# Weight pairs of the experts: seven block products in a row, then the pair's second product

## The chip, the cores and the metric

The kernel runs on 1 core of one Trainium2 chip. The metric is device microseconds (us) of that core for one execution; lower is better. TensorE (PE) multiplies, VectorE (DVE), ScalarE (ACT) and GpSimd (POOL) do the rest, SyncE (SP) issues DMAs. [...]

## The reference

Three stages, all in fp32: attention in which a query sees only keys of its own hash bucket (2 x 8 heads, 768 tokens, head size 64); a feed-forward layer `h = x @ w_in`, `g = h * tanh(softplus(h))`, `g @ w_out` (1536 tokens, 512 to 2048 to 512); and a mixture of 8 experts:

```python
for e in range(E):                       # E = 8
    h = np.maximum(x @ w1[e], 0.0)       # 1536 x 512 @ 512 x 1024
    ye = h @ w2[e]                       # 1536 x 1024 @ 1024 x 512
    out += P[:, e:e + 1] * ye            # P: gate probabilities, normalized 8 times
```

The change is in the last stage alone, in experts 1 to 7.

## The kernel before, in words

Every fp32 operand is split in two parts of type fp32r, hi and lo, and a product is three matmuls: hi with hi, hi with lo, lo with hi. Expert 0 runs with the feed-forward layer in an older scheme (lines 787 to 823: `up`, `down`). Experts 1 to 7 run in "units". A unit `u` is one half of the tokens (768, `g`), one expert `e`, and one of its four pairs `k` of 128-wide chunks of the hidden size; there are 2 x 7 x 4 = 56 units. Units 4n to 4n+3 are one expert on one half of the tokens.

The first product of a unit is a 2 x 2 block product (two chunks of the hidden size by two groups of 384 tokens) made by seven block products instead of eight (`PRODUCTS`, steps s = 0 to 6). Each is six matmuls of 128 x 128 by 128 x 384 (line 1122). They go to two PSUM banks, `bank[0]` and `bank[1]`, in turn: steps 0, 2, 4, 6 write the first, steps 1, 3, 5 the second, and only steps 0, 1 and 4 start a new sum. So what a step leaves in its bank must have been read before the step after next adds to the same bank. These reads are in `post(u, s)`: ACT copies step 0's result to `p1` (line 1152); DVE adds `p1` to the bank after steps 1 and 3 (`u`, `v`) and makes three of the four blocks of the hidden layer after steps 4, 5, 6 (`c22`, `c21`, `c12`, `total`, line 1142); block 11 is what step 2 leaves in the first bank, as it stands. For each block, ACT makes `hi = relu(c)` (`rounded`, line 1130) and DVE makes `lo = max(c, 0) - hi` (`rest`, line 1135). For block 11 both read the bank itself.

The second product of a unit takes the four hi/lo blocks as stationary operands and the unit's second weights (`w` or `ww`) as moving ones: 36 matmuls of 128 x 128 by 128 x 512 (`second_mm`, line 1185) into six PSUM banks `y`, one for each 128 tokens. A bank collects the four units of an expert; then `gather` (line 1195, DVE) adds it, times the gate probability, to `acc`. The last expert's results go out by DMA.

The order of the work is written out by hand at the end of the function. Before the change, the seven products of unit `u` alternate with the second product of unit `u - 1`: one block product, five or six matmuls of the second product, the next block product, and so on. Around each step stand `post`, the gathers that are due, and `jobs`: the conversions of the next weights (`unit_a`, `unit_s`, `unit_w`: hi on ACT, lo on POOL, and the sums of blocks on POOL), the scaling of `acc` by the first expert's probability in units 0 to 3 (`scale_first`), and the token-side factors for the second half of the tokens (`raw_next`, `parts_next`, units 18 to 28). An engine executes its instructions in the order in which they are issued here; PSUM tiles and SBUF tiles carry the waits between engines. In unit 0 there is no earlier unit, so its seven products stand in a row.

Of the kernel before, what the change touches and what calls it, by code (L numbers as in the profile page):

```python
# [24 lines left out]
NF = FE // P  # L25
# [27 lines left out]
def f32(t):  # L53
    return t[:].bitcast(F32)
# [3 lines left out]
def lsh_attention_moe_kernel(  # L58
# [13 lines left out]
    nc = tc.nc  # L72
# [24 lines left out]
    NU = 2 * (E - 1) * NF // 2  # L97

    def unit(u):
        g, x = divmod(u, NU // 2)  # L100
        return g, 1 + x // (NF // 2), x % (NF // 2)
# [667 lines left out]
    hps, hid, yps = {}, {}, {}  # L769
# [6 lines left out]
    def step(n):  # L776
        g, tb, i = steps[n]
        return g, tb, i, i == GROUPS[g][0], i == GROUPS[g][-1]
# [236 lines left out]
    t0 = start_e + 12  # L1015
# [31 lines left out]
    for i in range(RING_A + NX + 1, NW):  # L1047
        need = free[i - RING] + 1 if i >= RING else 0
        if NATT <= i < N64:
            nd = max(nd, free_dec.get(i - NDEC, 0))  # L1050
            for j in range(2):
                d = int(nd)
# [5 lines left out]
        t = nxt  # L1058
# [5 lines left out]
    for n in range(NST + LAG):  # L1064
# [6 lines left out]
        first = n >= LAG and step(n - LAG)[0] < NG and step(n - LAG)[4]  # L1071
# [16 lines left out]


    pool = lambda name, **kw: ctx.enter_context(tc.tile_pool(name=name, reuse_waits="tile", **kw))  # L1090
    wb_p, c_p, h_p = pool("wb", bufs=1), pool("c", bufs=1), pool("hid", bufs=2)
    ps_u = pool("ps_u", bufs=1, space=bass.MemoryType.PSUM)
    ps_z = pool("ps_z", bufs=1, space=bass.MemoryType.PSUM)
    wbuf.append(dict(
        s=wb_p.tile([P, 2, 1024], F32R, name="ws"), a=wb_p.tile([P, 2, 768], F32R, name="wa"),
# [3 lines left out]
    def weight(u, name, m, kc):  # L1099
        x, b = ("s", int(name[1]) - 1) if name[0] == "S" else ("a", ("A11", "A12", "A22").index(name))  # L1100
        return wbuf[u % 2][x][:, m, b * 256 + kc * P:b * 256 + (kc + 1) * P]

    def moving(u, name, m, kc):
        g = unit(u)[0]
        if name[0] == "T":
            return factor_t(g, int(name[1]), m, kc)
        return (xh, xl)[m][:, (int(name[1]) - 1) * (KC // 2) + kc, tokens(g, int(name[2]) - 1)]

    PRODUCTS = (
        ("A11", "B11", 0, True), ("S2", "T2", 1, True), ("A12", "B21", 0, False), ("S3", "T3", 1, False),  # L1110
        ("S1", "T1", 0, True), ("A22", "T4", 1, False), ("S4", "B22", 0, False),
    )
    bank, val, hid_u, y_t = {}, {}, {}, {}

    def product(u, s):
        a, b, x, first = PRODUCTS[s]
        if first:
            bank[x] = ps_u.tile([P, 512], F32, tag=f"u{(u + x) % 2}", name="u")[:, :HALF]
        n = 0
        for kc in range(KC // 2):  # L1120
            for m, mm in ((0, 0), (0, 1), (1, 0)):
                nc.tensor.matmul(bank[x], weight(u, a, m, kc), moving(u, b, mm, kc), start=(first and n == 0), stop=(n == 5), skip_group_check=not first)  # L1122
                n += 1

    def temp(tag, bufs=1):
        return c_p.tile([P, HALF], F32, tag=tag, name=tag, bufs=bufs)

    def rounded(u, c, src):
        hi = h_p.tile([P, HALF], F32R, tag=f"h{c}", name="gh")
        nc.scalar.activation(hi, src, AF.Relu)  # L1130
        hid_u[u, c] = [hi]

    def rest(u, c, src):
        lo = h_p.tile([P, HALF], F32R, tag=f"l{c}", name="gl")
        nc.vector.scalar_tensor_tensor(  # L1135
            out=lo, in0=src, scalar=0.0, in1=f32(hid_u[u, c][0]), op0=ALU.max, op1=ALU.subtract
        )
        hid_u[u, c].append(lo)

    def total(tag, x, y, bufs=1):  # L1140
        t = val[tag] = temp(tag if bufs == 1 else "c", bufs)
        nc.vector.tensor_add(t, x, y)  # L1142
        return t


    def post(u, s):
        a, b = bank[0], bank.get(1)
        if s == 0:
            if u:
                rest(u - 1, "12", val["c12"])  # L1150
            val["p1"] = temp("p1")
            nc.scalar.copy(val["p1"], a)
        elif s == 1:
            total("u", b, val["p1"])
        elif s == 2:
            rounded(u, "11", a)
            rest(u, "11", a)
        elif s == 3:
            total("v", b, val["p1"])
        elif s == 4:  # L1160
            rounded(u, "22", total("c22", a, val["v"], 2))
        elif s == 5:
            rounded(u, "21", total("c21", b, val["p1"], 2))
            rest(u, "22", val["c22"])
        else:
            rounded(u, "12", total("c12", a, val["u"], 2))
            rest(u, "21", val["c21"])

    def second(u):
        r = []  # L1170
        if u == NU - 1:
            order = [(c, t) for t in range(6) for c in (("11", "21") if t < 3 else ("22", "12"))]
        else:
            order = [(c, t) for c, t0 in (("11", 0), ("22", 3), ("21", 0), ("12", 3)) for t in range(t0, t0 + 3)]
        for n, (c, t) in enumerate(order):
            r += [(c, t, m, all(x[1] != t for x in order[:n]), all(x[1] != t for x in order[n + 1:])) for m in range(3)]
        return r

    def second_mm(u, c, t, m, first, last):
        g, e, k = unit(u)  # L1180
        if first and m == 0 and k == 0:
            y_t[t] = ps_z.tile([P, 512], F32, tag=f"z{t}", name="y")
        hi, lo = hid_u[u, c]
        y = wbuf[u % 2]["w"][:, int(m == 1), (int(c[0]) - 1) * 512:int(c[0]) * 512]
        nc.tensor.matmul(  # L1185
            y_t[t], (hi, hi, lo)[m][:, t % 3 * P:(t % 3 + 1) * P], y,
            start=(k == 0 and first and m == 0), stop=(k == NF // 2 - 1 and last and m == 2),
        )
        if last and m == 2 and k == NF // 2 - 1:
            done.append((g, e, t))  # L1190

    def gather(g, e, t):
        i = g * 6 + t
        dst = acc[:, i // KC, i % KC, :]
        nc.vector.scalar_tensor_tensor(
            out=dst, in0=y_t[t], scalar=prob[:, i, e:e + 1], in1=dst, op0=ALU.mult, op1=ALU.add
        )
        if e == E - 1:
            nc.sync.dma_start(out=out[i * P:(i + 1) * P, :], in_=dst)

    jobs = {}

    def job(u, s, f, *args):
        jobs.setdefault((u, s), []).append(lambda: f(*args))

    for u in range(NU):
        if u:
            job(u, 0, unit_w_hi, u)
            job(u, 0, unit_w_lo, u)
        if u == 0:  # L1210
            for s, f in enumerate((unit_a_hi, unit_a_lo, unit_s_hi, unit_s_lo)):
                job(u, s // 2, f, u + 1)
        elif u + 1 < NU:
            job(u, 1, unit_s, u + 1)
            job(u, 2, unit_a_hi, u + 1)
            job(u, 3, unit_s_hi, u + 1)
            job(u, 3, unit_s_lo, u + 1)
            job(u, 4, unit_a_lo, u + 1)
    for i in range(NT):
        job(i // 3, 1 + 2 * (i % 3), scale_first, i)  # L1220

    half = NU // 2

# [5 lines left out]
        parts_t(1, k, kc, held.pop((k, kc)))  # L1229

    for x in range(8):
        job(half - 10 + x, 3, raw_next, (1, 2, 4, 3)[x % 4], x // 4)
        if x % 4 == 2:
            job(half - 10 + x, 5, parts_next, 2, x // 4)
    for x, (u, s) in enumerate(((-1, 4), (-1, 5), (-1, 6), (0, 0), (0, 1), (0, 2))):
        job(half + u, s, parts_next, (3, 1, 4)[x // 2], x % 2)

    done = []
    for u in range(NU + 1):
        downs = second(u - 1) if u else []  # L1240
        for s in range(7):
            if u < NU:
                product(u, s)
            elif s == 0:
                rest(u - 1, "12", val["c12"])
            for x in downs[len(downs) * s // 7:len(downs) * (s + 1) // 7]:
                second_mm(u - 1, *x)
                if u == NU:
                    for d in done:
                        gather(*d)  # L1250
                    done.clear()
            if u < NU:
                post(u, s)
            for d in done:
                gather(*d)
            done.clear()
            for f in jobs.pop((u, s), []):
                f()
    assert not jobs, jobs.keys()


# [48 lines left out]
```

## Time and profile before

| what | value |
|---|---|
| runs before | 1592.61 us median of 3 (1591.12 to 1593.59) |
| span of the profiled execution, first to last instruction | 1591.4 us |
| TensorE busy | 1556.9 us, 98% of the span |
| TensorE weight loads | 1343.6 us, 84% (overlap the matmuls) |
| DVE, ACT, POOL busy | 54%, 40%, 55% |
| units of experts 1 to 7 | 704.0 us to about 1588 us of the span |

The profile gives no other time of its execution than the span. The units take more than half of it. A row of a list of instructions gives the start in us from the span's start, the duration, the engine, the line, what it writes and reads, and how many were merged in it; an idle time and its releaser stand in brackets.

### The profile page before, as it was taken

To read this page: it belongs to the slowest core of one execution; us is meant where nothing else is said; L and a number is where in the kernel's file an instruction comes from. 1 tells how busy PE (TensorE), PEld (TensorE's weight loads), DVE (VectorE), ACT (ScalarE), POOL (GpSimd) and SP (SyncE) were. 2 spreads that over 40 slices of the span, in tenths; PEclk is the share of its full clock that TensorE was granted. 3 is DMA by queue.
4 is the path that set the end of the run, shared out by engine and by line. 5 is a ranking of instruction groups with operands and counts; after the bars stand their busy time and mean duration, and the time that the engine had idled before them with its cause. 6 is when DMAs were issued, how large, how long until landed. Compare 5 with 4: busy or idle time off the path is not lost.

```text
span 1591.4 us, 20016 instructions
## 1 busy us (share of the span) xinstructions
PE 1556.9 (98%) x7407; PEld 1343.6 (84%) x7407; DVE 862.9 (54%) x1480; ACT 641.2 (40%) x1167; POOL 873.6 (55%) x697
## 2 busy tenths in 40 slices
PE   7889999999999999999999999999999999999999
PEld 5777777888888878888998998898898899899897
DVE  7999998687884222674433334455534243334243
ACT  4767766644333322223333333333333333333331
POOL 4787877442424240126565656666666666665652
PEclk9999999999999999999999999999999999999999
DMA  6645442022222010001222222222232222222221
GB/s 145 172 112 132 115 139 73 15 80 67 67 66 67 14 54 1 14 27 67 67 67 67 66 67 67 68 66 71 75 105 62 72 67 66 67 67 67 67 67 40
DMA packets 62641, 113.44 MB, mean 71 GB/s; under 512 B 18176, under 2 KB 18920, under 8 KB 62544
## 3 DMA queue, kind: packets, MB, share of 16 engines
q1 hardware_dynamic: 62544, 112.17, 23.9%
q8 instruction: 58, 0.95, 0.3%
q14 instruction: 39, 0.32, 0.1%
HBM read 89.22 MB, written 3.15 MB: 58 GB/s over the span
## 4 chain that ended last, share of the span: by engine, by line
PE 87%; DVE 10%; issue 1%; ACT 1%; DMA 1%; SPq 0%; DVEq 0%; ACTq 0%
PE y L1185 29%; PE u L1122 26%; PE y L823 12%; PE h L787 4%; PE h L789 4%; PE h L788 4%; PE pav L487 3%; DVE mx L399 3%; PE ps L385 1%; PE pst L437 1%; PE pst L438 1%; DVE col L404 0%; DVE bit L343 0%; DVE bit L337 0%; DVE xu L516 0%
## 5 line engine op out<-in xcount | busy, mean ns | idle before, releaser
L1185 PE MATMUL y<-w,gh 128*128 128x512 f32 x672 | 218.5, 393 | 0.0
L1185 PE MATMUL y<-ww,gh 128*128 128x512 f32 x672 | 218.1, 393 | 0.0
L1130 ACT ACTIVATE gh<-c 128x384 fp32r<-128x384 f32 x168 | 88.0, 526 | 278.4 <-DVE c L1142 278.4
L449 POOL TENSOR_TENSOR plo<-p,ph 128x384 fp32r<-128x384 f32 x128 | 142.3, 1122 | 68.9 <-ACT ph L446 37.9
L1185 PEld LDWEIGHTS y<-ww,gh 128*128 128x128 f32 x672 | 124.8, 188 | 18.2
L1185 PEld LDWEIGHTS y<-w,gh 128*128 128x128 f32 x672 | 124.8, 188 | 17.8
L1011 POOL TENSOR_TENSOR w<-stage,w 128x1024 fp32r<-128x1024 f32 x28 | 67.1, 2395 | 132.5 <-ACT w L1007 132.5
L1011 POOL TENSOR_TENSOR ww<-stage,ww 128x1024 fp32r<-128x1024 f32 x28 | 67.1, 2395 | 127.2 <-ACT ww L1007 127.2
L1185 PE MATMUL y<-w,gl 128*128 128x512 f32 x336 | 132.2, 394 | 0.0
L1185 PE MATMUL y<-ww,gl 128*128 128x512 f32 x336 | 132.2, 393 | 0.0
L1004 POOL TENSOR_TENSOR w<-sraw,w 128x1024 fp32r<-128x1024 f32 x28 | 67.4, 2407 | 107.3 <-ACT w L1000 107.3
L157 POOL TENSOR_TENSOR stage<-stage,sgn 128x512 f32<-128x512 f32 x32 | 46.6, 1455 | 119.8 <-DVE sgn L155 48.3
L1142 DVE TENSOR_TENSOR u<-u,p 128x384 f32<-128x384 f32 x56 | 31.2, 557 | 146.6 <-PE u L1122 146.6
L823 PE MATMUL y<-gh,w 128*128 128x512 f32 x336 | 110.2, 389 | 0.0
L443 ACT ACTIVATE p<-pst 128x384 f32<-128x384 f32 x192 | 92.9, 488 | 35.4 <-PE pst L438 31.2
L787 PE MATMUL h<-xh,w 128*128 128x512 f32 x252 | 99.5, 395 | 0.0
L788 PE MATMUL h<-xl,w 128*128 128x512 f32 x252 | 98.2, 390 | 0.0
L789 PE MATMUL h<-xh,w 128*128 128x512 f32 x252 | 98.1, 389 | 0.0
L1135 DVE SCALAR_TENSOR_TENSOR gl<-c,gh 128x384 fp32r<-128x384 f32 x168 | 94.2, 560 | 6.1 <-ACT gh L1130 0.2
L399 DVE TENSOR_REDUCE mx<-ps 128x1 f32<-128x768 f32 x95 | 89.9, 946 | 13.5 <-PE ps L385 12.9
L1130 ACT ACTIVATE gh<-u 128x384 fp32r<-128x384 f32 x56 | 27.5, 491 | 161.6 <-PE u L1122 161.6
L1135 DVE SCALAR_TENSOR_TENSOR gl<-u,gh 128x384 fp32r<-128x384 f32 x56 | 31.2, 557 | 109.8 <-ACT gh L1130 109.7
(246 smaller groups left out, 4060.7 us busy)
## 6 DMA issues: line engine op xcount, KB each, us to landing
stage<-in_w_dram SPq DMA_DIRECT2D x152, 512.0 KB
raw<-in_qk_dram SPq DMA_DIRECT2D x13, 384.0 KB
wx<-hi SPq DMA_DIRECT2D x20, 192.0 KB
vt<-in_v_dram SPq DMA_DIRECT2D x16, 192.0 KB
out_dram<-acc SPq DMA_DIRECT2D x12, 256.0 KB
zq<-hi SPq DMA_DIRECT2D x11, 192.0 KB
ak<-hi SPq DMA_DIRECT2D x11, 192.0 KB
zq<-lo SPq DMA_DIRECT2D x11, 192.0 KB
```

Of the source, the lines that this page charges most:

```text
L399: nc.vector.tensor_reduce(out=m[:, t:t + 1], in_=s_t[t][:, :, :HALF], axis=AX.XY, op=ALU.max)
L443: nc.scalar.activation(p_t[u, c], st_t.pop((u, c))[:, :HALF], AF.Exp, scale=0.125)
L449: (nc.gpsimd if e == "P" else nc.vector).tensor_sub(out, in0, in1)
L787: nc.tensor.matmul(t, wt[:, 0, f], xh[:, kc, c], start=(kc == 0), stop=False)
L788: nc.tensor.matmul(t, wt[:, 0, f], xl[:, kc, c], start=False, stop=False)
L789: nc.tensor.matmul(t, wt[:, 1, f], xh[:, kc, c], start=False, stop=(kc == KC - 1))
L823: nc.tensor.matmul(yps[j], x, y, start=(head and m == 0), stop=(tail and m == 2))
L1011: nc.gpsimd.tensor_sub(y[:, 1, :], t, f32(y)[:, 0, :])
L1122: nc.tensor.matmul(bank[x], weight(u, a, m, kc), moving(u, b, mm, kc), start=(first and n == 0), stop=(n == 5), skip_group_check=not first)
L1130: nc.scalar.activation(hi, src, AF.Relu)
L1135: nc.vector.scalar_tensor_tensor(out=lo, in0=src, scalar=0.0, in1=f32(hid_u[u, c][0]), op0=ALU.max, op1=ALU.subtract)
L1185: nc.tensor.matmul(y_t[t], (hi, hi, lo)[m][:, t % 3 * P:(t % 3 + 1) * P], y, start=(k == 0 and first and m == 0), stop=(k == NF // 2 - 1 a ...
```

## The change

The seven products of a unit stand in a row (`for s in range(NP1)`), each followed by its `post`; then come the 36 matmuls of the same unit's second product in four runs of nine. Block 11 is no longer turned into its lo part from the bank: DVE copies the bank to `c11` in SBUF (`tensor_copy`), and all four `rest` follow step 6. The order within the second product is changed, so that matmuls with hi parts of blocks 11 and 22 come first. Conversions of weights move: `unit_w` of the next unit to the front of a unit (step -1), the others behind the products (`NP1 + 1`), and so do `scale_first` and the token-side factors. The hidden blocks and the sums have one buffer in place of two.

```diff
-    wb_p, c_p, h_p = pool("wb", bufs=1), pool("c", bufs=1), pool("hid", bufs=2)
+    wb_p, c_p, h_p = pool("wb", bufs=1), pool("c", bufs=1), pool("hid", bufs=1)
...
         if s == 0:
-            if u:
-                rest(u - 1, "12", val["c12"])
             val["p1"] = temp("p1")
             nc.scalar.copy(val["p1"], a)
         elif s == 1:
             total("u", b, val["p1"])
         elif s == 2:
             rounded(u, "11", a)
-            rest(u, "11", a)
+            val["c11"] = temp("c11")
+            nc.vector.tensor_copy(val["c11"], a)
         elif s == 3:
             total("v", b, val["p1"])
         elif s == 4:
-            rounded(u, "22", total("c22", a, val["v"], 2))
+            rounded(u, "22", total("c22", a, val["v"]))
         elif s == 5:
-            rounded(u, "21", total("c21", b, val["p1"], 2))
-            rest(u, "22", val["c22"])
+            rounded(u, "21", total("c21", b, val["p1"]))
         else:
-            rounded(u, "12", total("c12", a, val["u"], 2))
-            rest(u, "21", val["c21"])
+            rounded(u, "12", total("c12", a, val["u"]))
+            for c in ("11", "22", "21", "12"):
+                rest(u, c, val["c" + c])
...
+        order = [(c, t, m) for c in ("11", "22") for t in tiles[c] for m in (0, 1)]
         if u == NU - 1:
...
+            for c, d in (("11", "21"), ("22", "12")):
+                for t in tiles[c]:
+                    order += [(c, t, 2)] + [(d, t, m) for m in range(3)]
         else:
...
+            order += [(c, t, 2) for c in ("11", "22") for t in tiles[c]]
+            order += [(c, t, m) for c in ("21", "12") for t in tiles[c] for m in (0, 1)]
+            order += [(c, t, 2) for c in ("21", "12") for t in tiles[c]]
...
+    for f in (unit_a_hi, unit_a_lo, unit_s_hi, unit_s_lo):
+        job(0, 0, f, 1)
+    for u in range(NU - 1):
+        job(u, -1 if u else 1, unit_w_hi, u + 1)
+        job(u, -1 if u else 1, unit_w_lo, u + 1)
+        if u + 2 < NU:
+            job(u, 0 if u else 1, unit_s, u + 2)
+            job(u, NP1 + 1, unit_a_hi, u + 2)
+            job(u, NP1 + 1, unit_s_hi, u + 2)
+            job(u, NP1 + 1, unit_a_lo, u + 2)
+            job(u, NP1 + 1, unit_s_lo, u + 2)
     for i in range(NT):
-        job(i // 3, 1 + 2 * (i % 3), scale_first, i)
+        job(i // 3, NP1 + 1 + i % 3, scale_first, i)
...
+    for x in range(6):
+        job(half - 1, NP1 - 1 + x // 2, parts_next, (3, 1, 4)[x // 2], x % 2)
...
+    for u in range(NU):
+        run_jobs(u, -1)
+        for s in range(NP1):
+            product(u, s)
+            post(u, s)
+            run_jobs(u, s)
+        downs = second(u)
+        for r in range(NRUN):
+            for x in downs[len(downs) * r // NRUN:len(downs) * (r + 1) // NRUN]:
+                second_mm(u, *x)
+                if u == NU - 1:
+                    settle()
+            settle()
+            run_jobs(u, NP1 + r)
```

`settle` issues the gathers that are due, `run_jobs` the jobs of a step.

## Rows read from the trace of the kernel before

**Rows 1.** The page: busy time and share of each engine.

```profile
PE 1556.9 (98%) x7407; PEld 1343.6 (84%) x7407; DVE 862.9 (54%) x1480; ACT 641.2 (40%) x1167; POOL 873.6 (55%) x697
```

**Rows 2.** Busy time by stretch: the units with both products, with PEclk and DMA.

```profile
712.86:1580.00 867.14, 867.14 (x4295) 781.26 (x4295) 351.61 (x614) 296.14 (x501) 541.28 (x433) 1.00 0.21 67
```

**Rows 3.** The chain that ended last: start, duration, engine, line, matmuls merged.

```profile
693.29 10.88 PE y L823 x48
704.17 2.12 PE u L1122 x12
...
727.38 1.39 PE y L1185 x6
729.82 1.16 PE y L1185 x5
732.04 1.16 PE y L1185 x5
...
1562.31 1.39 PE y L1185 x6
1578.06 9.58 PE y L1185 x42
```

**Rows 4.** Timeline of unit 0's products, steps 1 to 5, and a later conversion.

```profile
705.08 1.20 PE L1122 MATMUL u<-tw,w 128*128 128x384 f32 x6
705.28 0.48 ACT L1152 COPY p<-u 128x384 f32<-128x384 f32 x1 [8.32 <-PE u L1122]
...
706.12 0.33 PE L1122 MATMUL u<-xh,wx 128*128 128x384 f32 x1
...
706.39 0.56 DVE L1142 TENSOR_TENSOR u<-u,p 128x384 f32<-128x384 f32 x1 [1.48 <-PE u L1122]
...
707.16 1.23 PE L1122 MATMUL u<-tw,w 128*128 128x384 f32 x6
707.43 0.49 ACT L1130 ACTIVATE gh<-u 128x384 fp32r<-128x384 f32 x1
...
708.02 0.56 DVE L1135 SCALAR_TENSOR_TENSOR gl<-u,gh 128x384 fp32r<-128x384 f32 x1
...
708.64 1.01 PEld L1122 LDWEIGHTS u<-tw,w 128*128 128x128 f32 x6 [0.57 <-DVE gl L1135]
...
709.81 1.20 PE L1122 MATMUL u<-tw,wx 128*128 128x384 f32 x6
...
714.54 1.05 ACT L1007 CAST ww<-stage 128x1024 fp32r<-128x1024 f32 x1
```

**Rows 5.** DVE's groups by line and shape: busy us, mean ns, idle before.

```profile
L1195 DVE SCALAR_TENSOR_TENSOR acc<-y,prob,acc 128x512 f32<-128x512 f32 x84 | 59.1, 742 | 4.1 <-PE y L1185 4.1
...
L446 DVE CAST ph<-p 128x384 fp32r<-128x384 f32 x33 | 16.3, 493 | 3.4 <-ACT p L443 2.2 <-PE pav L487 0.9
...
L975 DVE TENSOR_TENSOR tw<-t,tw 128x384 fp32r<-128x384 f32 x14 | 11.8, 845 | 8.0 <-ACT tw L974 8.0
...
L854 DVE COPY lgs<-lg 16x512 f32<-16x512 f32 x3 | 2.0, 679 | 9.0 <-PE lg L849 9.0
```

**Rows 6.** The attention's PSUM tile `pav`: one reader; who waited for this tile's instructions (us, times).

```profile
L497 ACT COPY xu<-pav x32: 459/475/482, 39.9 to 300.0; 64x384 f32<-64x384 f32 x32
...
  ACT xu L497: 23.5, 21
```

**Rows 7.** Timeline: one instance of the two reads of `pav`.

```profile
85.80 0.58 DVE L495 STREAM_TRANSPOSE rs<-pav 64x384 f32<-64x384 f32 x1
...
86.42 0.47 ACT L497 COPY xu<-pav 64x384 f32<-64x384 f32 x1 [1.02 <-DVE rs L495]
```

**Rows 8.** Timeline: two gathers in a row, and the first gather of the last unit.

```profile
1022.77 1.40 DVE L1195 SCALAR_TENSOR_TENSOR acc<-y,prob,acc 128x512 f32<-128x512 f32 x2
...
1580.44 0.39 PE L1185 MATMUL y<-ww,gl 128*128 128x512 f32 x1
...
1580.87 0.75 DVE L1195 SCALAR_TENSOR_TENSOR acc<-y,prob,acc 128x512 f32<-128x512 f32 x1 [1.06 <-PE y L1185]
```

More of the change, by code (lines that the diff above doesn't have):

```diff
@@ L1138, in rest, with total @@
         hid_u[u, c].append(lo)
-    def total(tag, x, y, bufs=1):
-        t = val[tag] = temp(tag if bufs == 1 else "c", bufs)
+    def total(tag, x, y):
+        t = val[tag] = temp(tag)
         nc.vector.tensor_add(t, x, y)
@@ L1160, in post @@
         elif s == 4:
-            rounded(u, "22", total("c22", a, val["v"], 2))
+            rounded(u, "22", total("c22", a, val["v"]))
         elif s == 5:
-            rounded(u, "21", total("c21", b, val["p1"], 2))
-            rest(u, "22", val["c22"])
-        else:
-            rounded(u, "12", total("c12", a, val["u"], 2))
-            rest(u, "21", val["c21"])
+            rounded(u, "21", total("c21", b, val["p1"]))
+        else:
+            rounded(u, "12", total("c12", a, val["u"]))
+            for c in ("11", "22", "21", "12"):
+                rest(u, c, val["c" + c])
     def second(u):
-        r = []
+        tiles = {c: range(3 * int(c[1]) - 3, 3 * int(c[1])) for c in ("11", "22", "21", "12")}
+        order = [(c, t, m) for c in ("11", "22") for t in tiles[c] for m in (0, 1)]
         if u == NU - 1:
-            order = [(c, t) for t in range(6) for c in (("11", "21") if t < 3 else ("22", "12"))]
-        else:
[L1174 to L1177, printed above, removed]
+            for c, d in (("11", "21"), ("22", "12")):
+                for t in tiles[c]:
+                    order += [(c, t, 2)] + [(d, t, m) for m in range(3)]
+        else:
+            order += [(c, t, 2) for c in ("11", "22") for t in tiles[c]]
+            order += [(c, t, m) for c in ("21", "12") for t in tiles[c] for m in (0, 1)]
+            order += [(c, t, 2) for c in ("21", "12") for t in tiles[c]]
+        return [
+            (c, t, m, all(x[1] != t for x in order[:n]), all(x[1] != t for x in order[n + 1:]))
+            for n, (c, t, m) in enumerate(order)
+        ]
     def second_mm(u, c, t, m, first, last):
         g, e, k = unit(u)
-        if first and m == 0 and k == 0:
+        if first and k == 0:
             y_t[t] = ps_z.tile([P, 512], F32, tag=f"z{t}", name="y")
@@ L1186, in second_mm @@
             y_t[t], (hi, hi, lo)[m][:, t % 3 * P:(t % 3 + 1) * P], y,
-            start=(k == 0 and first and m == 0), stop=(k == NF // 2 - 1 and last and m == 2),
+            start=(k == 0 and first), stop=(k == NF // 2 - 1 and last),
         )
-        if last and m == 2 and k == NF // 2 - 1:
+        if last and k == NF // 2 - 1:
             done.append((g, e, t))
@@ L1204, in job @@
         jobs.setdefault((u, s), []).append(lambda: f(*args))
[L1206 to L1218, printed above, removed]
+    NP1 = len(PRODUCTS)
+    NRUN = 4
+    for f in (unit_a_hi, unit_a_lo, unit_s_hi, unit_s_lo):
[9 more added lines that the diff above has]
+            job(u, NP1 + 1, unit_s_lo, u + 2)
     for i in range(NT):
-        job(i // 3, 1 + 2 * (i % 3), scale_first, i)
+        job(i // 3, NP1 + 1 + i % 3, scale_first, i)
     half = NU // 2
@@ L1231, in lsh_attention_moe_kernel, with settle, run_jobs @@
     for x in range(8):
-        job(half - 10 + x, 3, raw_next, (1, 2, 4, 3)[x % 4], x // 4)
+        job(half - 10 + x, NP1 + 1, raw_next, (1, 2, 4, 3)[x % 4], x // 4)
         if x % 4 == 2:
-            job(half - 10 + x, 5, parts_next, 2, x // 4)
-    for x, (u, s) in enumerate(((-1, 4), (-1, 5), (-1, 6), (0, 0), (0, 1), (0, 2))):
-        job(half + u, s, parts_next, (3, 1, 4)[x // 2], x % 2)
+            job(half - 10 + x, NP1 + 2, parts_next, 2, x // 4)
+    for x in range(6):
+        job(half - 1, NP1 - 1 + x // 2, parts_next, (3, 1, 4)[x // 2], x % 2)
     done = []
[L1239 to L1258, printed above, removed]
+    def settle():
+        for d in done:
+            gather(*d)
+        done.clear()
+    def run_jobs(u, s):
+        for f in jobs.pop((u, s), []):
+            f()
+    for u in range(NU):
[12 more added lines that the diff above has]
+            run_jobs(u, NP1 + r)
     assert not jobs, jobs.keys()
```

## The prediction, made before the changed kernel was run

> **What bounds the kernel now.** I read the page first: TensorE is busy 98% of the span, no other engine over 55% [rows 1]. [...] A unit begins every 15.753 us (727.38 to 1562.31 us is 53 units) [rows 3]. Inside it, five matmuls of the second product take 1.16 us (0.231 each), and the next five begin 2.22 us later, so a block product between them takes 1.06 us [rows 3]. Where 512-wide matmuls stand long in a row, 48 take 10.88 us, 0.2267 each, and of the last 42 the 36 behind the last switch take 9.58 - 6 x 0.231 = 8.19 us [rows 3]. Two block products in a row without a wait take 2.08 us, 1.04 each (705.08 to 707.16) [rows 4]; 12 right behind a switch take 2.12 [rows 3]. A switch between the two kinds thus costs some 0.04 us, and the kernel now makes fourteen per unit.
>
> Fourth, the timeline of unit 0, which has no earlier unit's second product: it is the changed order of products already, in small, and it is there that I look for gaps.
>
> **The change part by part.**
>
> *Grouping.* A unit's TensorE work becomes 7 x 1.04 + 0.04 + 8.19 = 15.51 us against 15.753: 0.243 less. Between the start of unit 1's products and the last second product there are 55 such units: -13.4 us. Bounds: nothing, if the spacing stays as it is; -17, if the switches left cost nothing (15.44 us per unit).
>
> *Cover taken from the reads of the banks.* Before, a reader of a bank had the next product and ten matmuls, some 3.4 us, until the bank was written again. Now it has one product, 1.04 us, and the weight load of the writer wants to start when the sixth matmul does, 0.87 us after the product. Unit 0 shows a read by DVE: the product ended at 706.12, the add began 0.27 later and took 0.56; a weight load behind such a DVE instruction starts 0.06 after it (708.02 + 0.56 to 708.64) [rows 4]. That is 0.89: 0.02 late. I take 0.05 per unit for the two steps of this kind (s = 3 behind `u`, s = 6 behind `c22`): +2.8 us; 0 to 0.1 per unit as bounds.
>
> *The copy of block 11.* After step 2 two engines read the first bank: ACT for hi, then DVE, now by a copy that needs nothing of ACT's result. Do they run side by side? The attention has such a pair: DVE transposes one half of `pav`, ACT copies the other half into another tile. ACT waited for DVE 21 times of 32 at this tile, 23.5 us in all [rows 6], and an instance shows it: DVE 85.80 to 86.38, ACT from 86.42 after 1.02 us idle [rows 7]. Neither reads what the other writes; what they share is the bank. So reads of a bank by two engines go one after the other, in program order, 0.04 apart, and the copy will stand behind the ReLU. [...]
>
> The chain after step 2: ReLU from +0.27 for 0.49 (707.43, product end 707.16) [rows 4], DVE from +0.80, copy 0.55, weight load of step 4 at +1.41. The copy is worked out from DVE's copy of 512 fp32 out of PSUM, 0.679 us [rows 5], by columns between 0.51 (all of it scaled) and 0.56 (like the add); the farthest rows, an SBUF source with 0.493 [rows 5], would give 0.06 less. In unit 0 the same chain, with `rest` as its third link and DVE 0.06 late, put that load at +1.48, and steps 3 and 4 took 709.81 - 707.16 = 2.65 us for 2.08 [rows 4]: 0.57 lost. At +1.41 it is 0.50. In 42 of the 55 units: +21.0 us. Bounds 0.40 to 0.57 per unit: +17 to +24.
>
> *Gathers.* An expert's six banks now all finish with the last six matmuls of a fourth unit, so its six gathers stand in a block in DVE's queue, ahead of the next unit's `u`. The first can begin 0.43 us after the start of its bank's last matmul (1580.44 to 1580.87) [rows 8], which is 6 x 0.227 = 1.36 before the end: at -0.93. Two take 1.40 [rows 8], one 0.742 [rows 5], so they follow at 0.66 and DVE is free at +3.03; `u` could have begun at 2.11 + 0.27 = 2.38. It ends at 3.59, the load of step 3 starts at 3.65 in place of 2.98, and 0.63 us is lost by the measure of unit 0. While TensorE waits there, the copy of block 11 catches up (3.95 to 4.50, load 4.56, wanted at 4.6), so 0.63 takes the place of 0.50. 13 times: +8.2 us. Bounds 0.50 (the gathers hidden behind the copy's stall) to 1.0.
>
> *Conversions and the rest.* `unit_w` of the next unit opens a unit on ACT, in front of `p1`. It may start when the second product before has read its buffer, about +0.2, and takes 1.05 [rows 4]; `p1` then runs 1.29 to 1.77, and the load of step 2 can start at 1.83, wanted at 1.94. Hidden, with 0.1 to spare; each 0.1 beyond costs 5.5 us. The four `rest` and `c12` take five times 0.56 behind the products, ready by +3.1, while the first lo part is wanted after 12 matmuls (2.7 us) and it is done at 1.4: hidden by the second product. The other conversions have 8.2 us of second product and a unit more before they are read. The single buffers are written again only after the second product that read them: nothing. `parts_next` of the change of token half puts six subtractions of 0.85 us [rows 5] (1.13 in the worst stretch) behind the rests of unit 27, ahead of its gathers, and makes `u` 1 to 2.6 us later still: +2, once. In unit 0 the `scale_first` that held up its products goes, but three conversions now stand before the ReLU on ACT: about +0.1 together.
>
> *Sum* against the span of 1591.4: -13.4 + 2.8 + 21.0 + 8.2 + 2.0 + 0.1 = +20.7, span 1612.1. The runs' median lies 1.2 above that span; with the same 1.2 the time is 1613.3, said as 1613 us.
>
> **The rivals.**
>
> *A: the copy runs beside the ReLU.* For it: neither needs the other. Against it: the 21 waits [rows 6]. The 21.0 go; 55 x (0.05 - 0.243) + 8.2 + 2.0 - 0.5 = -0.9: 1592 us, no change, between 1586 and 1597. It decides from 0.08 us per unit: a copy that makes the load later than that turns no change into slower. This is the only case not slower that I can work out.
>
> *B: the spacing does not depend on the neighbours,* so grouping gives nothing: 1613 + 13 = 1626 us. Against it: 0.231 and 0.2267 in the same profile [rows 3]. [...]
>
> *C: `p1` comes late,* since ACT's conversion starts later than +0.2. For it: only 0.1 us to spare. At 0.2 beyond that, 55 x 0.2 = 11: 1624 us.
>
> **How the numbers follow.** Forecast 0.78, A 0.12, B 0.05, C 0.05. The forecast's own range is 1602 to 1622: the copy's bounds (-4, +3), the gathers (-2, +5), the grouping's lower end (-4), the half's change. From 1600 to 1624 lie some 0.74 of the forecast's 0.78 and C's 0.05, about 0.8 in all, and A and B are left out; that is the range. What a measurement of this kernel tells from no change is about 0.2%, 3.2 us. Slower by more than that: the forecast, B, C and a little of A, 0.89. Within it 0.07, faster 0.04, both from A.
>
> **What would show it.** In the profile after: products 0 to 2 at 1.04 us each; between the first matmuls of steps 3 and 5 some 2.6 us in place of 2.08, with a wait of TensorE for the DVE copy `c11`, whose start is at the ReLU's end + 0.04; the second product at 0.227 per matmul; a unit every 16.0 us; six gathers in a block at every fourth unit and the wait there at step 3, for `u`. Wrong if the copy starts with the ReLU (A), if 512-wide matmuls still stand 0.231 apart (B), if step 2 waits for ACT (C), or if the gathers begin later than 0.9 us before the end of a second product.

## The result, and the profile after

| | median us | runs | against the kernel before, 95% interval |
|---|---|---|---|
| before | 1591.86 | 4 (1590.89 to 1593.59) | |
| after | 1606.03 | 4 (1605.9 to 1608.38) | 1.0089 [1.0076, 1.0103] |

The change costs 14.2 us, where the forecast was 20.7: slower, by the mechanism forecast, and inside the range; the forecast cost was about 1.4 times the measured one. The profiled execution after has a span of 1606.6 us against 1591.4, so the trace shows 15.2; 15.0 of it lies in the units.

The page after, busy time and share, answers to [rows 1]:

```profile
PE 1560.1 (97%) x7407; PEld 1335.7 (83%) x7407; DVE 957.3 (60%) x1536; ACT 642.4 (40%) x1167; POOL 875.9 (55%) x697
```

The same 7407 matmuls; DVE has 56 instructions more, the copies, and is busy 94 us longer. The stretch of the units, one row for [rows 2]:

```profile
712.86:1594.00 881.14, 869.13 (x4290) 771.94 (x4289) 446.89 (x668) 295.68 (x499) 541.78 (x433) 1.00 0.21 66
```

In this stretch TensorE, which had no gap before (busy 867.14 of 867.14 us, [rows 2]), now has 12 us of 881 without a matmul. The stalls worked out below are longer: a matmul's record (0.33 us) lasts past the start of the next where none waits (0.17 us, a sixth of 1.04), and so covers the first part of a gap. The granted clock is 1.00 in both stretches. The chain that ended last shows the new order and its price; it answers to [rows 3] (start, duration, engine, line, count):

```profile
1002.18 8.20 PE y L1189 x36
1010.38 3.16 PE u L1122 x18
1014.75 3.43 PE u L1122 x18
1018.76 2.97 DVE gl L1135 x4
1025.42 3.12 DVE acc L1199 x5
1029.89 4.46 PE u L1122 x24
1034.35 8.20 PE y L1189 x36
```

The second product takes 8.20 us for 36 matmuls (8.19 forecast). The first unit's chain runs 18 matmuls (steps 0 to 2) from 1010.38 to 1013.54, and goes on at 1014.75: between them step 3 (1.04 us) and a wait. In the next unit, behind an expert's last, the chain runs through four `rest` and the gathers on DVE, and the wait is one step earlier. The timeline of the first one, against [rows 4]:

```profile
1012.33 0.33 PE L1122 MATMUL u<-xh,wa 128*128 128x384 f32 x1
...
1012.59 0.56 DVE L1142 TENSOR_TENSOR u<-u,p 128x384 f32<-128x384 f32 x1 [2.57 <-PE u L1122]
...
1013.21 1.07 PEld L1122 LDWEIGHTS u<-tw,ws 128*128 128x128 f32 x6
1013.37 1.23 PE L1122 MATMUL u<-tw,ws 128*128 128x384 f32 x6
1013.62 0.49 ACT L1130 ACTIVATE gh<-u 128x384 fp32r<-128x384 f32 x1 [1.60 <-PE u L1122]
...
1014.14 0.56 DVE L1155 COPY c<-u 128x384 f32<-128x384 f32 x1 [0.99 <-ACT gh L1130]
...
1014.75 1.33 PE L1122 MATMUL u<-tw,ws 128*128 128x384 f32 x6 [0.16 <-DVE c L1155]
...
1015.93 1.20 PE L1122 MATMUL u<-tw,wa 128*128 128x384 f32 x6
```

The first three rows are the read of step 1's result: its product ends at 1012.33, the add into `u` begins 0.26 us later, and the weight load that waits for it comes 0.06 after its end, in time. Step 2's product ends where step 3 starts, at 1013.37. ACT's ReLU ends at 1014.11, DVE, idle for 0.99 us, begins its copy 0.03 later, and step 4 starts at 1014.75, 0.05 after the copy. Steps 3 and 4 take 2.56 us instead of 2.08. And the timeline behind an expert's last unit, against [rows 8]:

```profile
1025.34 4.03 DVE L1199 SCALAR_TENSOR_TENSOR acc<-y,prob,acc 128x512 f32<-128x512 f32 x6
...
1029.30 0.54 DVE L1142 TENSOR_TENSOR u<-u,p 128x384 f32<-128x384 f32 x1
...
1029.89 2.38 PE L1122 MATMUL u<-tw,w 128*128 128x384 f32 x12 [0.37 <-DVE u L1142]
1030.13 0.56 DVE L1155 COPY c<-u 128x384 f32<-128x384 f32 x1 [0.29 <-ACT gh L1130]
```

Six gathers in a block, 4.03 us; `u` begins when they are through, 3.09 us into the unit (3.03 forecast). Steps 3 and 4 then run as 12 without a gap: the copy's wait is covered. The list of who waited for whom, from 720 us on, so behind the first unit, has two rows with a weight load of TensorE (waiter, releaser, us in total, times, longest):

```profile
PEld u L1122 <- DVE c L1155: 20.4, 42, 0.5
PEld u L1122 <- DVE u L1142: 9.3, 13, 1.5
```

Before, the same list had no row of TensorE. These are the two terms of the sum: the copy in 42 units and the gathers in 13.

### The profile page after: what moved, and what is told of

Read it like the earlier page. It is cut to its first block, busy times and chain, and to the rows that moved or that the text cites. A ratio compares the mean times of both kernels' runs of the same rounds, so it can differ in the third digit from the quotient of the medians.

```text
span 1606.6 us, 20403 instructions
## 1 busy us (share of the span) xinstructions
PE 1560.1 (97%) x7407; PEld 1335.7 (83%) x7407; DVE 957.3 (60%) x1536; ACT 642.4 (40%) x1167; POOL 875.9 (55%) x697
## 4 chain that ended last, share of the span: by engine, by line
PE 80%; DVE 14%; ACT 2%; DMA 2%; issue 1%; SPq 0%; POOL 0%; ACTq 0%; DVEq 0%
PE y L1189 27%; PE u L1122 21%; PE y L823 12%; PE h L787 4%; PE h L789 4%; PE h L788 4%; DVE acc L1199 3%; PE pav L487 3%; DVE mx L399 2%; DVE c L1155 2%; ACT gh L1130 1%; PE ps L385 1%; PE pst L437 1%; PE pst L438 1%; DVE bit L343 0%
## 5 line engine op out<-in xcount | busy, mean ns | idle before, releaser
L1135 DVE SCALAR_TENSOR_TENSOR gl<-c,gh 128x384 fp32r<-128x384 f32 x224 | 168.5, 814 | 0.0
L1189 PE MATMUL y<-ww,gh 128*128 128x512 f32 x672 | 163.4, 391 | 0.0
L1189 PE MATMUL y<-w,gh 128*128 128x512 f32 x672 | 162.6, 391 | 0.0
L987 POOL TENSOR_TENSOR wa<-stage,wa 128x512 fp32r<-128x512 f32 x28 | 38.5, 1374 | 109.6 <-ACT wa L982 85.8
L1122 PE MATMUL u<-tw,w 128*128 128x384 f32 x420 | 85.8, 344 | 8.5 <-DVE u L1142 5.1
L1122 PE MATMUL u<-tw,ws 128*128 128x384 f32 x420 | 88.0, 344 | 4.6 <-DVE c L1155 4.6
L1122 PEld LDWEIGHTS u<-tw,w 128*128 128x128 f32 x420 | 72.5, 188 | 17.5 <-DVE u L1142 9.3
```

What stands on the lines that cost most here:

```text
L1135: nc.vector.scalar_tensor_tensor(out=lo, in0=src, scalar=0.0, in1=f32(hid_u[u, c][0]), op0=ALU.max, op1=ALU.subtract)
L1189: nc.tensor.matmul(y_t[t], (hi, hi, lo)[m][:, t % 3 * P:(t % 3 + 1) * P], y, start=(k == 0 and first), stop=(k == NF // 2 - 1 and last),)
```

## The experiments

The theory: two engines read a PSUM bank one after the other, by waits that come with the program's PSUM tiles, and in the tight order this puts the ReLU in front of the read that step 4 waits for. The rivals: the copy's own latency, a wait for data, or the grouping itself. Ratios are against runs of the kernel before on the same chip; "the stage" is the stretch from the first block product to the start of the last matmul, 883.2 us before and 898.2 after, which leaves out what varies ahead of the units: their first product begins between 701.8 and 704.4 us in these profiles, with the same code in front of it.

**DVE copies first, and the ReLU reads the copy.**

```diff
-            rounded(u, "11", a)
             val["c11"] = temp("c11")
             nc.vector.tensor_copy(val["c11"], a)
+            rounded(u, "11", val["c11"])
```

> The changed kernel (1606.0 us) with step 2's two reads of the first bank in the other order: DVE copies the bank to c11, and the ReLU of block 11 reads c11. Theory (reads of a bank by two engines go in series, and the ReLU in front of the copy is what makes step 4 late): the bank is free after one read, the load of step 4 at +0.87 us where it is wanted, steps 3 and 4 take 2.08 us in place of 2.54 in 42 units, so -0.46 x 42 = -19.5: 1586.5 us, below the kernel before. At the 13 units behind gathers nothing changes. Rival (the time of step 4 is the copy's own latency on DVE, whoever reads first): 1606 us, steps 3 and 4 still 2.5 us.

Measured: 1587.08 us, 0.9962 [0.995, 0.9975]; the stage is 20.3 us shorter than after the change, 1.4 of it in unit 0. Of the two waits one is left:

```profile
PEld u L1122 <- DVE u L1142: 9.3, 13, 1.5
```

One read of the bank, 0.56 us, fits into a product of 1.04 us here; two, 0.49 and 0.56 us, did not. The rival falls: DVE's copy is as long as before (0.56 us on average in the profile of both edits below, which has the same order) and no longer in the way.

**Both reads from the bank, DVE's first.** This tells whether the gain came from the order or from the number of reads.

```diff
-            rounded(u, "11", a)
             val["c11"] = temp("c11")
             nc.vector.tensor_copy(val["c11"], a)
+            rounded(u, "11", a)
```

> The changed kernel (1606.0 us) with DVE's copy of the bank first and the ReLU second, both still reading the bank, so neither has data of the other. Theory (two engines read one bank in series, in program order): the chain is as long as before, 0.25 + 0.56 + 0.04 + 0.49 + 0.06 = 1.40 us after step 2, steps 3 and 4 take 2.54 us and the time is 1606 us. Rival 1 (the reads may overlap, and the first edit's gain came from DVE starting first): 1587 us as with the ReLU reading c11. Behind gathers the copy now waits for u, and the ReLU behind it: +0.5 x 13 = up to 6 us more, 1612.

Measured: 1606.15 us, 1.0084 [1.007, 1.0098], as after the change. The timeline of one unit:

```profile
1012.20 1.23 PE L1122 MATMUL u<-tw,ws 128*128 128x384 f32 x6
1012.39 0.56 DVE L1154 COPY c<-u 128x384 f32<-128x384 f32 x1 [0.42 <-PE u L1122]
...
1013.05 0.49 ACT L1130 ACTIVATE gh<-u 128x384 fp32r<-128x384 f32 x1 [2.20 <-DVE c L1154]
...
1013.59 1.31 PE L1122 MATMUL u<-tw,ws 128*128 128x384 f32 x6 [0.17 <-ACT gh L1130]
```

ACT's input has been there since the product ended, at 1012.20, and ACT is idle; it starts at 1013.05, 0.10 after DVE's copy ends, though it reads nothing that DVE wrote. The order is turned round, and the stall has the same size. The extra loss behind gathers did not come: the units there are as long as after the change.

**Block 11's lo part from the bank, as in the kernel before.**

```diff
             rounded(u, "11", a)
-            val["c11"] = temp("c11")
-            nc.vector.tensor_copy(val["c11"], a)
+            rest(u, "11", a)
...
-            for c in ("11", "22", "21", "12"):
+            for c in ("22", "21", "12"):
```

> The changed kernel with block 11's lo part made by DVE from the bank behind the ReLU, as in the kernel before, and no copy. Theory (the copy waits for the ReLU by the bank anyhow, so that it needs nothing of its result gives nothing): 1606.0 us within 1, steps 3 and 4 still 2.54 us. Rival (the copy runs at least partly beside the ReLU and saves time against the old lo part): 0.2 us or more per unit slower, 1614 us.

Measured: 1611.62 us, 1.0117 [1.0103, 1.0131]: neither number. An ordinary unit's products take 7.79 us on average against 7.77, as the theory has it: an instruction that needs the ReLU's result starts when one that doesn't need it did (0.03 us behind the ReLU's end, 1029.93 to 1029.96 us in one unit, as the copy did after the change). The time is 5.6 us longer than after the change, but the profiled execution after was the slowest of its four, and from profile to profile the stage is 3.8 us longer; what else the time holds stays open. Of the 3.8, 3.2 lie in one place, the first unit of the second half of the tokens (11.1 us of products in place of 7.9). The timeline just before it:

```profile
1151.25 3.73 DVE L975 TENSOR_TENSOR tw<-t,tw 128x384 fp32r<-128x384 f32 x2 [1.21 <-ACT tw L974]
...
1151.85 2.72 POOL L1004 TENSOR_TENSOR ws<-sraw,ws 128x1024 fp32r<-128x1024 f32 x1
...
1154.90 4.03 DVE L1198 SCALAR_TENSOR_TENSOR acc<-y,prob,acc 128x512 f32<-128x512 f32 x6
...
1158.86 0.54 DVE L1142 TENSOR_TENSOR u<-u,p 128x384 f32<-128x384 f32 x1
...
1159.45 3.00 PE L1122 MATMUL u<-tw,w 128*128 128x384 f32 x9 [1.94 <-DVE u L1142]
```

With DVE's list 0.6 us shorter, two subtractions from SBUF fell beside a long POOL instruction and took 3.73 us, where after the change they took 1.84. The gathers began 1.4 us later than there and `u` with them, and TensorE's wait for `u` grew by 1.6 us. That is half of the 3.2. The other half is the clock: behind this wait of some 2 us, nine matmuls take 3.00 us, 0.32 from one to the next in place of 0.173, and by stretch (PEclk is the third number from the end):

```profile
1160.00:1163.00 3.00, 3.00 (x11) 3.00 (x11) 0.56 (x1) 0.00 (x0) 0.79 (x2) 0.50 0.86 247
1164.00:1167.00 3.00, 3.00 (x17) 2.70 (x16) 2.06 (x5) 1.90 (x4) 0.00 (x0) 1.00 0.00 0
```

The granted clock was 0.50 there, and 1.00 again behind it. In the profiles before and after it is 1.00 in every 15 us of the units. No run shows why it fell here.

**A second ReLU of the bank.**

```diff
             rounded(u, "11", a)
+            nc.scalar.activation(temp("dup"), a, AF.Relu)
             val["c11"] = temp("c11")
```

> The changed kernel (1606.0 us) with a second ReLU of the same bank into an unused tile between the ReLU of block 11 and DVE's copy; the output is the same. Theory (the copy waits for ACT's last read of the bank): the load of step 4 comes 0.40 us later, +0.40 x 42 = 16.8 us, and behind gathers, where the copy has some 0.1 us to spare, +0.3 x 13 = 4: 1627 us; steps 3 and 4 together 2.95 us in place of 2.54. Rival (the copy waits for something else, or only for its own data): 1606 us.

Measured: 1625.21 us, 1.0207 [1.0193, 1.0221], 19 us more than the change for 21 expected. An ordinary unit is 0.38 longer on average, one behind gathers 0.22.

**Gathers spread over the second product.**

```diff
-        if u == NU - 1:
+        if unit(u)[2] == NF // 2 - 1:
             for c, d in (("11", "21"), ("22", "12")):
```

> The changed kernel with the order of the last unit's second product used in every fourth unit, so that an expert's six banks finish 0.9 us apart from the 16th matmul on and the gathers no longer stand in a block. Theory (the gathers' stall takes the place of the copy's, and does not add to it): behind an expert the products fall from 7.92 to 7.78 us, 12 times, and from 8.82 once: -0.14 x 12 - 1.0 = -2.7: 1603.3 us. Rival (the gathers' 0.6 us adds to the copy's stall): -0.6 x 13 = -8: 1598 us. Rival 2 (the hidden lo parts come too late for this order): 1606 us or more, with waits of TensorE for gl.

Measured: 1605.73 us, 1.008 [1.0067, 1.0094], which the time alone can't tell from the change. The trace can: the products behind an expert are 7.78 us as everywhere, the stage is 1.7 shorter, and TensorE now waits for the copy in 54 units, not in 42:

```profile
PEld u L1122 <- DVE c L1155: 26.0, 54, 0.5
PEld u L1122 <- DVE u L1142: 2.1, 3, 1.5
```

So one stall had covered the other. The 1.0 us for unit 4 was not won: there the wait stays, 8.80 us of products.

**Both edits.**

> Both edits: DVE's copy first, and the gathers spread. Theory: no read of a bank and no gather is late; a unit is 7.31 + 8.20 = 15.51 us, against 15.75 before. From the first edit's 1586.5 the gathers' 0.61 us falls away 12 times, and 1.5 once: 1577.7 us, 0.9% below the kernel before; this is the price of the grouping alone (-13 us of 1591.9). Rival (grouping saves nothing without its stalls): 1590 us or more.

Measured: 1579.11 us, 0.9921 [0.9907, 0.9934]. The stage is 12.0 us shorter than before and an ordinary unit takes 15.53 us: the grouping is worth 0.22 us in each of 55 units, 12.3 us where 13.4 were forecast, and the two stalls had eaten it twice. (The 12.0 also hold 1.5 us of unit 0, whose wait went too, against 2.0 us of waits that are left in units 4, 20 and 24.)

**What is left of waits.** To both edits comes:

```diff
-        job(i // 3, NP1 + 1 + i % 3, scale_first, i)
+        job(i // 4, NP1 + i % 4, scale_first, i)
...
-        job(half - 10 + x, NP1 + 1, raw_next, (1, 2, 4, 3)[x % 4], x // 4)
+        ux = half - (11, 10, 8, 7, 6, 4, 3, 2)[x]
+        job(ux, NP1 + 1, raw_next, (1, 2, 4, 3)[x % 4], x // 4)
...
-            job(half - 10 + x, NP1 + 2, parts_next, 2, x // 4)
+            job(ux, NP1 + 2, parts_next, 2, x // 4)
```

> The kernel with DVE's copy first and the gathers spread (1579.1 us), with the scaling by the first expert's probability moved to units 0 to 2, four each, and the token-side factors kept out of the fourth units. Theory (what is left of waits sits in DVE's queue behind gathers in units 4, 20 and 24, 1.5 and twice 0.27 us): 1577.1 us, and no wait of TensorE behind the first unit. Rival (the scaling is late wherever it stands): 1579 us.

Measured: 1579.13 us, 0.9917 [0.9904, 0.9931]. In time it can't be told from the version before it; its stage is 1.6 us shorter, and TensorE's wait behind the first unit is one of 0.2 us. This and the version before it beat both kernels. What held up unit 4 stands in the trace after the change, in DVE's list: the last scaling (line 903) between the gathers and `u`.

```profile
768.20 4.04 DVE L1199 SCALAR_TENSOR_TENSOR acc<-y,prob,acc 128x512 f32<-128x512 f32 x6
772.16 0.97 DVE L903 TENSOR_SCALAR acc<-acc,prob 128x512 f32<-128x512 f32 x1
773.06 0.55 DVE L1142 TENSOR_TENSOR u<-u,p 128x384 f32<-128x384 f32 x1
```

**The conversion that opens a unit, twice.** The sum had it at nothing, hidden by 0.1 us.

```diff
     def unit_w_hi(u):
         nc.scalar.copy(wbuf[u % 2]["w"][:, 0, :], staged["u", u, 1].rearrange("p c n -> p (c n)"))
+        nc.scalar.copy(wbuf[u % 2]["w"][:, 0, :], staged["u", u, 1].rearrange("p c n -> p (c n)"))
```

> The changed kernel with the hi conversion that opens a unit on ACT (1.05 us, in front of p1) made twice, the second writing the same values again. Theory (hidden now, with 0.1 us to spare): p1 comes 0.95 later, step 2's load 0.8 late; +0.8 us in 42 units, +0.65 behind gathers, where the wait for u goes and that for the copy returns: +42: 1648 us, step 1 or 2 longer by 0.8. Rival (more than 1 us to spare, since p1 does not stand behind it): 1606 us.

Measured: 1647.06 us, 1.0345 [1.0331, 1.0359]; the cover is as thin as worked out, and what it covers is real (waits up to 1600 us of a span of 1645.6):

```profile
PEld u L1123 <- ACT p L1150: 42.9, 53, 0.8
PEld u L1123 <- DVE c L1156: 23.1, 52, 0.5
```

**Grouping without giving up the cover.** The kernel before, with its second product in three runs of 12.

```diff
-            for x in downs[len(downs) * s // 7:len(downs) * (s + 1) // 7]:
+            for x in (downs[6 * s:6 * s + 12] if s % 2 == 0 and s < 6 else ()) if u < NU else downs[...]:
```

> The kernel before (1591.9 us), its second product of the earlier unit given out in three runs of 12 matmuls, behind steps 0, 2 and 4, in place of seven runs of five or six. Six switches per unit in place of fourteen, and each read of a bank still has 12 matmuls and a product, or a product alone for step 0, as cover. Theory (a pair of switches costs 0.045 us): 15.44 + 3 x 0.045 = 15.575 us per unit, -0.178 x 55 = -9.8: 1582 us, without a wait of TensorE. Rival (only runs of 36 and 42 bring the spacing down, or it depends on something else than switches): 1590 us or more.

Measured: 1596.4 us, 1.0024 [1.0015, 1.0034]: the expectation fell, in two ways. Six of the units 18 to 25 lost 8.1 us, since `raw_next` at step 3 now stood on DVE just in front of `c22`. And without those a unit takes 15.66 us, not 15.575. With the token-side factors moved:

```diff
-        job(half - 10 + x, 3, raw_next, (1, 2, 4, 3)[x % 4], x // 4)
+        job(half - 10 + x, 0, raw_next, (1, 2, 4, 3)[x % 4], x // 4)
```

> The kernel before with its second product in three runs of 12, as e8, and the token-side factors of units 18 to 25 (which stood in front of c22 on DVE and cost 8.1 us in six units of e8) moved to step 0, behind which 12 matmuls cover them. Theory as mended by e8 (a switch costs as long as its following run lets it: 0.073 us per pair with runs of 12, 0.045 with runs of 5 and 6): 15.66 us per unit against 15.753, -0.093 x 55 = -5.1: 1587.7 us of 1592.8. Rival (0.045 per pair, and something else made e8 slow): 1583 us.

Measured: 1588.44 us, 0.9973 [0.9962, 0.9984], with one wait of TensorE of 0.5 us left behind the first unit. The chain of this kernel:

```profile
1082.98 2.76 PE y L1185 x12
1085.74 3.17 PE u L1122 x18
1088.91 2.76 PE y L1185 x12
```

12 matmuls of the second product take 2.76 us, 0.04 more than 12 x 0.2267, as much as 36 do (8.20 - 8.16); five in the kernel before took 1.16, 0.02 to 0.03 more than 1.133. By their starts in the traces, the first nine of a run of 12 or 36 stand 0.224 to 0.236 us apart and those behind them 0.227. So in these traces the slow spacing behind a switch lasts some nine 512-wide matmuls, a run of five pays only part of it, and the saving does not go by the number of switches.

## Why the prediction was right, point by point

- **Grouping**, -13.4: right, a little too much. Without the stalls an ordinary unit takes 15.53 us (15.51 forecast), -12.3. The rival in which the spacing does not depend on the neighbours is out: with the stalls gone the two edits run 12 us of stage below the kernel before, and 0.2278 us per matmul in the second product stands beside 0.231.
- **Reads of `u` and `c22`**, +2.8: too much. Step 2 takes 1.042 us and step 5 1.040, so the two cost nothing that can be seen. The read of `u` began 0.27 us after the product, as taken, that of `c22` 0.20, and the weight load behind `u` came at 0.88 where 0.87 was wanted (five matmuls of 0.173): that is no more than the 0.02 worked out, and the 0.05 was put on top of it without a row.
- **The copy of block 11**, +21.0: right in mechanism, 0.45 per unit for 0.50, 18.7 us (15.98 us for an ordinary unit with the stall, 15.53 without). Shown by the order turned round (same time), by the lo part that needs the ReLU (same unit), by one read less (the stall gone) and by one read more (0.38 worse). Where the timelines show both reads of this bank, they stand one after the other: DVE's copy began 0.03 us behind the end of ACT's ReLU after the change, ACT's ReLU 0.10 behind the end of DVE's copy with the order turned round. But the waits that keep them apart are the program's, so no run shows what the chip would do without them. For the same reason the 21 waits at `pav` show less than the prediction took from them: 20 of them, 23.2 us, were for DVE, and there the two engines read different halves of the partitions (64 each). They show how this program orders the reads of a tile, and that is what the forecast needed.
- **Gathers**, +8.2: 0.60 in 12 units and 1.5 in unit 4, 8.7 us; that they take the place of the copy's stall is shown by the 42 and 54 waits. The 0.9 us more of unit 4 is not the gathers': the prediction put the moved scaling (`scale_first`, line 903) at nothing there, and the last of it stood between the gathers and `u`; with it moved to units 0 to 2, that wait went.
- **Conversions**, nothing: right, and shown to be only just hidden.
- **Change of token half**, +2.0: not there (7.92 us, as behind every expert), since the six subtractions took 3.8 us and not 5.1 or more. The term was not wrong in kind: with one instruction less on DVE it appeared, as 1.6 us of wait, and the granted clock of 0.50 behind that wait cost 1.6 more, which no term had.
- **Unit 0**, +0.1: 8.73 us for 8.85, -0.1.

The terms as measured, -12.3 + 0 + 18.7 + 8.7 + 0 - 0.1, make 15.0, which is what the stage shows. So the sum came out 5.7 too high. Three terms that were mis-sized make 7.1 of it, the two tight reads (2.8), the copy (2.3) and the change of half (2.0), and unit 0 makes 0.2; the grouping (1.1) and the gathers with the scaling (0.5) were off in the other direction and hid 1.6 of it, which is luck.

## What to carry to other kernels

Where matmuls are grouped, count the reads of each bank between its last write and its next, put them in series whichever engine makes them where the program's waits do so (here 0.03 to 0.10 us apart), and compare the sum with the TensorE work left between: here one read of 0.56 us fits under 1.04 us, and 0.49 and 0.56 do not. A read that only feeds another engine can go through the first reader's copy in SBUF (here 1587.08 us in place of 1606.03). Before a gain is put down to fewer switches, look how long the slow spacing lasts (some nine matmuls here), and look what else stands in the queue of the engine that frees the bank: a block of gathers cost 0.6 us each time, the copy 0.45.

## What the runs showed of the hardware that was not expected

DVE instructions whose operands all lie in SBUF took up to 5.5 times as long beside a POOL instruction (line 965: 0.55 us before, 2.74 after; line 903: 0.47 to 2.63 us in the trace after), and which ones did moved with the schedule. DVE's groups in the units, before (mean ns is the number behind the busy us):

```profile
L966 DVE TENSOR_TENSOR t<-t,tt 128x384 f32<-128x384 f32 x4 | 10.6, 2652 | 0.1
...
L965 DVE TENSOR_TENSOR tt<-xl 128x384 f32<-128x384 f32 x4 | 2.2, 551 | 0.0
```

and after:

```profile
L1135 DVE SCALAR_TENSOR_TENSOR gl<-c,gh 128x384 fp32r<-128x384 f32 x224 | 168.5, 814 | 0.0
...
L1155 DVE COPY c<-u 128x384 f32<-128x384 f32 x55 | 30.7, 558 | 45.5 <-ACT gh L1130 45.5
...
L965 DVE TENSOR_TENSOR tt<-xl 128x384 f32<-128x384 f32 x4 | 11.0, 2744 | 0.0
...
L966 DVE TENSOR_TENSOR t<-t,tt 128x384 f32<-128x384 f32 x4 | 2.2, 559 | 0.1
```

Line 966 became fast, line 965 slow (and line 970, from 0.56 to 2.64 us), and the timeline after shows its neighbour:

```profile
1006.30 2.71 POOL L1004 TENSOR_TENSOR w<-sraw,w 128x1024 fp32r<-128x1024 f32 x1
...
1006.68 2.75 DVE L965 TENSOR_TENSOR tt<-xl 128x384 f32<-128x384 f32 x1
```

Here DVE's instruction ends at 1009.43 us, POOL's at 1009.01. `rest`, now behind the products and partly beside POOL, rose from 0.56 to 0.81 us; instructions with a PSUM operand stayed as long as before (line 1142 and the copy at 0.56, the gathers at 0.74). The scaling of line 903, which reads one tensor in SBUF, took 0.47 or 0.48 us where POOL ran nothing beside it and 2.61 to 2.63 beside POOL's line 1004, four times, in the trace after. All this cost little here because the second product covers the four `rest`; where such an instruction stood ahead of `u`, in unit 4 (0.97 us, line 903) and in the run with block 11's lo part from the bank (3.73 us, line 975), it came out as a wait of TensorE (its weight load's, 1.5 and 2.25 us). No run varied it alone, so its cause is not shown.
